# Turning and ReLU of the smallest expert blocks moved to the vector engine, with their first product by column halves (fp32 sigmoid attention and mixture of experts, one core)

## The chip, the core and the metric

The kernel runs on one core of a Trainium2 chip. Five engines work beside each other, each with an instruction queue of its own that it takes in order: TensorE (PE; its weight loads are counted apart as PEld), VectorE (DVE), ScalarE (ACT), GpSimd (POOL) and SyncE (SP), which here issues the plain transfers. An engine waits for another through semaphores. Matmul results land in PSUM, in banks of 512 fp32 numbers for each of 128 partitions; everything else lies in SBUF. The metric is the device time of one execution in microseconds (us), lower is better.

## What is computed

```python
scores = 1/sqrt(64) * q @ k.T - log(448)      # 8 x 12 heads, 448 x 64
x = sigmoid(scores) @ v                       # -> 3584 tokens x 768
out = x.copy()
for tokens with x @ w_skip > 0:
    e    = argmax(x @ w_gate)                 # one of 8 experts
    gate = softmax(x @ w_gate)[e]
    out  = x + gate * (relu(x @ w1[e]) @ w2[e])   # 768 -> 1024 -> 768
```

All of it is fp32.

## The kernel before

Up to about 322 us the kernel does attention and routing; the first two blocks of 128 tokens of the fullest expert are done at its end. Then a loop takes the rest block by block, one expert after the other. Which blocks there are is known only at run time, so each turn of the loop branches, on each engine, to one of four arms: FULL (a block of up to 128 tokens), SPLIT (the same, and the weights of the next expert, which lie there raw, are turned into pairs of a high and a low part on the side), HALF (up to 64 tokens) and FEW (up to 32 tokens). With the data used here there are 14 blocks in the loop, five of them FEW: four come behind a FULL block and one behind a SPLIT block; the last FEW block is the last of the program.

FULL and SPLIT form each product as three products of high and low parts. `gemm1` (L516) gives the hidden layer in `ph`, `relu` (L525, ACT) takes it to `hs`, `turn_h` (L530, PE) and `split_h` (L535 ACT, L536 DVE) turn and split it, `gemm2` (L543) gives the result in `py`: 48 matmuls of 384 columns, for each of 8 slices of the hidden layer three products, each for the two output halves. `weigh_sum` (L1316, DVE, twice) scales the halves of `py` by the gate into `ys`, `put` (POOL, L1281 to L1296 and the scatter, L570) adds them to the output in memory, `advance` (L1306, L1308, L1309, DVE) moves the block's records on. SPLIT has beside these the weights' conversions (L1225, L1231 on ACT; L1228, L1234 on DVE); the last four of L1234 stand at its very end, behind `advance`.

FEW uses the raw weights. It reads the tokens' transposed rows (`xf`) as weights of PE, 32 columns wide, so that four matmuls work side by side in four column groups of the array, and streams the expert's weights. In the order of the program:

- `take_rec` (L1313, DVE): copies the next block's record.
- First product (L1381, PE): 6 row tiles x 4 groups, 256 columns each, all in one bank `ph[0]`. Group g holds the hidden layer's columns 256g to 256g+255 of the 32 tokens in partitions 32g to 32g+31. An fp32 matmul counts as two passes: 48.
- ReLU (L1398, ACT) in two halves of 128 columns, from `ph[0]` into `hs`.
- `load_w1`: SP starts the transfers of the next expert's first weights. `turn_x` (L492): six PE transposes of the next block's rows, into `pxt`. `fetch` (POOL, L1259 to L1265 and the gathers L560 and L1111): gathers rows and record of the block after.
- Turn of the hidden layer: two PE transposes of 128 x 128 (L1407) into `pht[0]` and `ph[1]`, two copies on ACT (L1409) into `ht`.
- `ready_x`: `hi_x` (L498, ACT), `whole_x` (L1093, ACT), `lo_x` (L502, DVE) prepare the next block's rows out of `pxt`. `shift` (L1277, DVE) moves the list of coming blocks.
- Second product (L1381, PE): 4 rounds of 4 matmuls of 384 columns, one for each group; groups 0 and 1 make output half 0, groups 2 and 3 half 1, each from half of the hidden layer. All land in one bank, `py[:, 0, :]`.
- Sums: ACT scales groups 0 and 2 (L1434), DVE scales groups 1 and 3 and adds (L1436). Then `put` and `advance`.

A scheduler doesn't move instructions here: within an arm each engine's instructions stand in the order of the code.

Of the kernel before, what the change touches and what calls it, by code (L numbers as in the profile page):

```python
# [10 lines left out]
F32 = mybir.dt.float32  # L11
# [4 lines left out]
ALU = mybir.AluOpType  # L16
# [7 lines left out]
def kernel(  # L24
# [513 lines left out]
    def gemm2(j, hh, hl, py):  # L538
        h, m = divmod(j, 4)
        js = slice(m * P, (m + 1) * P)  # L540
        for n, (a, w) in enumerate(((hh, wh2), (hh, wl2), (hl, wh2))):
            for o in range(2):
                last = nc.tensor.matmul(  # L543
                    py[:, o, :H2],
                    a[h][:, js],
                    w[j][:, o * H2 : (o + 1) * H2],
                    start=(j == 0 and n == 0),
                    stop=(j == NK2 - 1 and n == 2),
                )
        return last  # L550

# [585 lines left out]
    pxt = [ps_b.tile([P, 512], F32, tag="b", name="pxt0"), new_t("pxt1")]  # L1137
    for h in range(2):
        turn_x(xc, h, pxt[h])
        hi_x(h, pxt[h], xh)  # L1140
# [58 lines left out]
    py = new_s("py")  # L1199
# [118 lines left out]
    def block(i, last):  # L1318
# [48 lines left out]
        for o in range(2):  # L1367
            weigh_sum(ys[:, o * H2 : (o + 1) * H2], py[:, o, :H2], recs[:, 0, 0:1])
# [6 lines left out]
    def few(i):  # L1375

        nx = next_expert(ds(i + 2, 1))
        take_rec()
# [11 lines left out]
        Q1 = FF // 4  # L1390
        for j in range(NK1):
            for g in range(4):
                s = slice((g % 2) * Q1, (g % 2 + 1) * Q1)
                quarter(ph[0], g, Q1, xf[:, j, :SM], raw1[j][g // 2][:, s], j, NK1)
        turned = (pht[0], ph[1])
        parts = [slice(c * P, (c + 1) * P) for c in range(2)]
        for s in parts:
            nc.scalar.activation(hs[:, s], ph[0][:, s], AF.Relu)  # L1398
# [6 lines left out]
        ht4 = ht[:, : 8 * SM].rearrange("p (c g t) -> p c g t", c=2, g=4)  # L1405
        for s, p in zip(parts, turned):
            nc.tensor.transpose(p[:, :P], hs[:, s], ident)  # L1407
        for s, p in zip(parts, turned):
            nc.scalar.activation(ht[:, s], p[:, :P], AF.Copy)  # L1409
# [3 lines left out]
        for n, j in enumerate((0, 2, 1, 3)):  # L1413
            for g in range(4):
                o, h = g // 2, g % 2
                m = j + h * (NK2 // 2)
                quarter(
                    py[:, 0, :],
                    g,
                    H2,  # L1420
                    ht4[:, j % 2, 2 * h + j // 2, :],
                    raw2[m][:, o * H2 : (o + 1) * H2],
# [135 lines left out]
```

## Time and profile before

| | |
|---|---|
| time, median of 3 runs | 525.33 us (525.12 to 526.49) |
| time of the profiled execution | 528.89 us |
| its span, first to last instruction | 526.5 us |
| mean granted PE clock | 0.993 |
| busy: PE, DVE, ACT, POOL | 97%, 56%, 53%, 49% |
| PE's matmuls at L1381, first products of the 5 FEW blocks | 14.1 us |
| PE's matmuls at L1381, second products of the 5 FEW blocks | 14.5 us |
| ReLU of the FEW blocks on ACT (L1398), 10 instructions | 2.2 us |

Times of the trace count from the first instruction. The chain of waits goes back from the last instruction, at each step to what released it. A timeline lists an engine's instructions with start, length, and in brackets the engine's idle time ahead and what ended it. "L1381" is a line of the kernel, and names such as `py<-raw,ht` are its tiles. Groups give busy time and, behind it, the mean ns of one instruction. The five FEW blocks begin on PE at 403.3, 429.5, 455.7, 481.8 and 507.4 us.

### The profile page before, as it was taken

What the parts mean: (1) busy time and instruction counts of PE and PEld (TensorE: products, weight loads), DVE (VectorE), ACT (ScalarE), POOL (GpSimd) and SP (SyncE); (2) the same over time, 40 slices, a digit from 0 to 9 for tenths busy, and PEclk for the clock granted to TensorE, in tenths of its full rate; (3) what the DMA queues carried; (4) which work ended last, traced back from release to release, by engine and by line L of the source; (5) the groups of instructions that cost most, each with busy time, mean ns of one, the idle gap of its engine ahead of it and who ended that gap; (6) DMA issues with size and microseconds to landing.
All of it is one profiled execution on the core that took longest, in us unless ns stands there. A gap on an engine that the chain in (4) does not pass through costs nothing.

```text
span 526.5 us, 14852 instructions
## 1 busy us (share of the span) xinstructions
PE 509.3 (97%) x4793; PEld 333.8 (63%) x4794; DVE 296.0 (56%) x721; ACT 280.8 (53%) x485; POOL 257.1 (49%) x404
## 2 busy tenths in 40 slices
PE   8999999999999999999999999999999999999991
PEld 6664545545545446555446988948577777778870
DVE  4556857658667677586775952962122222259422
ACT  5776776767767667677664212932212323268231
POOL 4523553533566766766663341553324444445643
PEclk9999999999999999999999999999999999999997
DMA  8998787897999999999865024979393959595941
GB/s 207 218 240 192 167 184 158 180 179 169 195 206 232 220 196 212 211 205 211 188 117 114 2 92 133 386 220 336 88 390 113 348 202 348 188 341 217 356 150 32
DMA packets 140288, 107.21 MB, mean 204 GB/s; under 512 B 97099, under 2 KB 112731, under 8 KB 140240
## 3 DMA queue, kind: packets, MB, share of 16 engines
q1 hardware_dynamic: 134000, 97.66, 70.0%
q0 software_dynamic: 4576, 8.65, 7.2%
q8 instruction: 30, 0.49, 0.4%
q10 hardware_dynamic: 1664, 0.26, 0.3%
q14 instruction: 18, 0.15, 0.1%
HBM read 98.49 MB, written 17.56 MB: 220 GB/s over the span
## 4 chain that ended last, share of the span: by engine, by line
PE 91%; DVE 3%; ACT 1%; DMA 1%; SPq 1%; issue 1%; POOLq 0%; ACTq 0%; POOL 0%; DVEq 0%
PE s L212 24%; PE pa L240 22%; PE ph L516 11%; PE py L543 11%; PE b_ph L516 3%; PE b_py L543 3%; PE py L1381 3%; PE ph L1381 2%; PE py L1448 2%; PE ph L1448 2%; PE pxt L492 2%; PE pl L280 1%; PE pht L530 1%; SPq L263 1%; PE pg L297 1%
## 5 line engine op out<-in xcount | busy, mean ns | idle before, releaser
L232 ACT ACTIVATE at<-s,bias 128x896 f32<-128x896 f32 (+1 forms) x191 | 173.4, 913 | 81.2 <-PE s L212 70.7
L212 PE MATMUL s<-x 64*64 64x448 f32 (+1 forms) x1528 | 163.9, 497 | 0.9 <-DVE sel L407 0.6
L240 PE MATMUL pa<-at,v 64*64 64x448 f32 (+1 forms) x1536 | 161.7, 489 | 0.0
L176 POOL COPY kq<-kq 32x896 f32<-32x896 f32 (+1 forms) x96 | 87.3, 910 | 92.2 <-DMA kq<-in_q_dram 52.2
L212 PEld LDWEIGHTS s<-x 64*64 64x64 f32 x1528 | 78.3, 191 | 54.3 <-issue 28.0
L240 PEld LDWEIGHTS pa<-at,v 64*64 64x64 f32 x1536 | 60.7, 133 | 56.3 <-issue 48.7
L194 DVE STREAM_TRANSPOSE x<-kq 128x448 f32<-128x448 f32 x94 | 80.9, 934 | 4.9 <-POOL kq L176 4.9
L250 DVE TENSOR_TENSOR xt<-xt,pa 128x448 f32<-128x448 f32 x48 | 29.7, 619 | 53.9 <-ACT xt L669 53.9
L414 POOL DMA_INDIRECT lst<-rec,idx x32 | 31.5, 983 | 17.6 <-DVE xt L250 5.4
L486 POOL TENSOR_TENSOR wl<-wr,wh 128x384 fp32r<-128x384 f32 (+1 forms) x28 | 31.2, 1124 | 15.1 <-DVE wh L485 9.2
L255 DVE STREAM_TRANSPOSE y<-xt 128x448 f32<-128x448 f32 x48 | 31.0, 645 | 5.5 <-DMA out_dram<-y 4.1
L570 POOL DMA_INDIRECT out_dram<-ys,rp x15 | 23.7, 1578 | 16.6 <-issue 8.4
L536 DVE TENSOR_TENSOR hl<-pht,hh 128x512 fp32r<-128x512 f32 x14 | 9.7, 689 | 37.0 <-ACT hh L535 30.0
L543 PE MATMUL py<-wh,hh 128*128 128x384 f32 x112 | 29.8, 347 | 0.0
L525 ACT ACTIVATE hs<-ph 128x512 f32<-128x512 f32 x14 | 8.3, 596 | 39.7 <-PE ph L516 31.7
L543 PE MATMUL py<-wh,hl 128*128 128x384 f32 x112 | 28.8, 338 | 0.0
L543 PE MATMUL py<-wl,hh 128*128 128x384 f32 x112 | 28.7, 337 | 0.0
L502 DVE TENSOR_TENSOR xl<-pxt,xh 128x384 fp32r<-128x384 f32 x30 | 15.3, 551 | 20.4 <-ACT xf L1093 8.3
L516 PE MATMUL ph<-wl,xh 128*128 128x512 f32 x84 | 26.6, 403 | 0.0
L669 ACT ACTIVATE xt<-pa 128x448 f32<-128x448 f32 x48 | 25.7, 536 | 0.8 <-PE pa L240 0.8
L516 PE MATMUL ph<-wh,xh 128*128 128x512 f32 x84 | 25.7, 402 | 0.0
L1316 DVE TENSOR_SCALAR ys<-py,recs 128x384 f32<-128x384 f32 (+1 forms) x18 | 10.4, 611 | 25.8 <-PE py L543 20.7
(275 smaller groups left out, 691.6 us busy)
## 6 DMA issues: line engine op xcount, KB each, us to landing
raw<-in_moe_w_dram SPq DMA_DIRECT2D x64, 768.0 KB
v<-in_v_dram SPq DMA_DIRECT2D x48, 256.0 KB
out_dram<-y SPq DMA_DIRECT2D x192, 56.0 KB
kq<-in_k_dram SPq DMA_DIRECT2D x46, 224.0 KB
kq<-in_q_dram SPq DMA_DIRECT2D x46, 224.0 KB
wr<-in_moe_w_dram SPq DMA_DIRECT2D x12, 256.0 KB
wr<-in_moe_w_dram SPq DMA_DIRECT2D x16, 192.0 KB
lst<-fill SPq DMA_DIRECT2D x4, 464.0 KB
```

The source lines that it names most:

```text
L176: nc.gpsimd.tensor_copy(a[BT:, :, :, :BT], a[:BT, :, :, BT:])
L194: nc.vector.transpose(xs[:, n].rearrange("p (r j) -> p j r", j=NJ), t.rearrange("p (j d) -> p j d", d=D)[:, :, :BT],)
L212: nc.tensor.matmul(sc[m * D : (m + 1) * D, j, : qs.stop - qs.start], xs[r, 0, first::NR7], xs[r, 1, qs], start=True, stop=True,)
L232: nc.scalar.activation(at[:, :, :n], sc[:, :, :n], AF.Sigmoid, bias=bias, scale=SCALE)
L240: nc.tensor.matmul(pa[j * D : (j + 1) * D, r, qs], vt[rs, j, r + c if c < 3 else 3 * (1 - r), :], at[rs, j, : qs.stop - qs.start], start=( ...
L250: nc.vector.tensor_tensor(x, x, pa[:, 1, :S], op=ALU.add)
L255: nc.vector.transpose(y, xts[b][:, hp, :])
L414: put = nc.gpsimd.indirect_dma_start(out=lst[:, :], out_offset=bass.IndirectOffsetOnAxis(ap=idx[:, c : c + 1], axis=0), in_=rec[:, c, :], ...
L486: nc.gpsimd.tensor_tensor(lo, r, hi, op=ALU.subtract)
L516: nc.tensor.matmul(ph[h], a[:, j * P : (j + 1) * P], w[j][h], start=(n == 0), stop=(n == len(t) - 1),)
L543: last = nc.tensor.matmul(py[:, o, :H2], a[h][:, js], w[j][:, o * H2 : (o + 1) * H2], start=(j == 0 and n == 0), stop=(j == NK2 - 1 and n ...
L1381: nc.tensor.matmul(dst[g * SM : (g + 1) * SM, :n], a, w, start=(j == 0), stop=(j == most - 1), tile_position=(0, g * SM),)
```

## The change

1. FEW's first product goes by column halves c: c=0 takes the first 512 columns of the hidden layer into `ph[0]`, c=1 the rest into `ph[1]`. Each of the 48 matmuls has 128 columns, read as 4 strips of 32 that lie 128 apart, so that group g holds the strips g, g+4 and so on. Blocks of 32 x 32 within `hs` are then all that has to be turned.
2. After each half DVE does the ReLU (a maximum with 0) out of PSUM and turns the 128 x 128 tile in blocks of 32 x 32 into `ht`. The two PE transposes, ACT's ReLU and ACT's copies go. `take_rec` stands behind the first half's turn.
3. The second product takes the slices of the hidden layer in another order, so that its first two rounds need half c=0 alone.
4. `py` is two tiles of one bank each in place of one of two banks. In FEW, groups 0 and 2 (read by ACT) write `py0`, groups 1 and 3 (read by DVE) `py1`. HALF uses `py0` alone. In FULL and SPLIT they are the two output halves, and the last slice of `gemm2` does half 0's three matmuls first.
5. `pxt` is one tile of two banks; at the end of the stage ahead of the loop both halves are turned first and taken by `hi_x` then.

The lines of the changed kernel stand 3 to 10 further down: `gemm2` L546, `take_rec` L1321, FEW's matmuls L1388, ReLU L1411, turn L1412, sums L1444 and L1446, `weigh_sum` L1324, the conversions L1242.

```diff
@@ -538,16 +538,22 @@
     def gemm2(j, hh, hl, py):
         h, m = divmod(j, 4)
         js = slice(m * P, (m + 1) * P)
-        for n, (a, w) in enumerate(((hh, wh2), (hh, wl2), (hl, wh2))):
-            for o in range(2):
-                last = nc.tensor.matmul(
-                    py[:, o, :H2],
-                    a[h][:, js],
-                    w[j][:, o * H2 : (o + 1) * H2],
-                    start=(j == 0 and n == 0),
-                    stop=(j == NK2 - 1 and n == 2),
-                )
+        parts = [(n, o) for n in range(3) for o in range(2)]
+        if j == NK2 - 1:
+            parts.sort(key=lambda t: t[1])
+        for n, o in parts:
+            a, w = ((hh, wh2), (hh, wl2), (hl, wh2))[n]
+            last = nc.tensor.matmul(
+                half_y(py, o),
+                a[h][:, js],
+                w[j][:, o * H2 : (o + 1) * H2],
+                start=(j == 0 and n == 0),
+                stop=(j == NK2 - 1 and n == 2),
+            )
         return last
+
+    def half_y(py, o):
+        return py[o][:, :H2] if isinstance(py, list) else py[:, o, :H2]
 
     def finish(ys, py, gate, x):
         for o in range(2):
@@ -1134,9 +1140,11 @@
     turn0(1)
     for j in range(2, NK2 - 3):
         gemm2(j, hh0, hl0, py)
-    pxt = [ps_b.tile([P, 512], F32, tag="b", name="pxt0"), new_t("pxt1")]
+    pxt2 = new_s("pxt")
+    pxt = [pxt2[:, h, :] for h in range(2)]
     for h in range(2):
         turn_x(xc, h, pxt[h])
+    for h in range(2):
         hi_x(h, pxt[h], xh)
     for h in range(2):
         whole_x(h, [slice(j, j + 1) for j in range(3)])
@@ -1196,7 +1204,7 @@
     raw2 = [raw2g[j // 2][:, j % 2, :] for j in range(NK2)]
 
     ph = [new_t(f"ph{h}") for h in range(2)]
-    py = new_s("py")
+    py = [new_t("py0"), ps_b.tile([P, 512], F32, tag="b", name="py1")]
     pht2 = new_s("pht")
     pht = [pht2[:, h, :] for h in range(2)]
 
@@ -1365,7 +1373,7 @@
         else:
             shift(dve)
         for o in range(2):
-            weigh_sum(ys[:, o * H2 : (o + 1) * H2], py[:, o, :H2], recs[:, 0, 0:1])
+            weigh_sum(ys[:, o * H2 : (o + 1) * H2], half_y(py, o), recs[:, 0, 0:1])
         put(P, last)
         advance(1 if last else 2)
         if last:
@@ -1375,7 +1383,6 @@
     def few(i):
 
         nx = next_expert(ds(i + 2, 1))
-        take_rec()
 
         def quarter(dst, g, n, a, w, j, most):
             nc.tensor.matmul(
@@ -1387,39 +1394,42 @@
                 tile_position=(0, g * SM),
             )
 
-        Q1 = FF // 4
-        for j in range(NK1):
-            for g in range(4):
-                s = slice((g % 2) * Q1, (g % 2 + 1) * Q1)
-                quarter(ph[0], g, Q1, xf[:, j, :SM], raw1[j][g // 2][:, s], j, NK1)
-        turned = (pht[0], ph[1])
-        parts = [slice(c * P, (c + 1) * P) for c in range(2)]
-        for s in parts:
-            nc.scalar.activation(hs[:, s], ph[0][:, s], AF.Relu)
+        split = [slice(c * P, (c + 1) * P) for c in range(2)]
+        for c, s in enumerate(split):
+            for j in range(NK1):
+                cols = raw1[j][c].rearrange("p (m g f) -> p g m f", g=4, f=SM)
+                for g in range(4):
+                    quarter(
+                        ph[c].rearrange("p (m f) -> p m f", f=SM)[:, :4],
+                        g,
+                        4,
+                        xf[:, j, :SM],
+                        cols[:, g],
+                        j,
+                        NK1,
+                    )
+            nc.vector.tensor_scalar(hs[:, s], ph[c][:, :P], 0.0, None, op0=ALU.max)
+            nc.vector.transpose(ht[:, s], hs[:, s])
+            if c == 0:
+                take_rec()
         for h in range(2):
             for g in range(2):
                 load_w1(g, h, nx)
         for h in range(2):
             turn_x(xn, h, pxt[h])
         fetch()
-        ht4 = ht[:, : 8 * SM].rearrange("p (c g t) -> p c g t", c=2, g=4)
-        for s, p in zip(parts, turned):
-            nc.tensor.transpose(p[:, :P], hs[:, s], ident)
-        for s, p in zip(parts, turned):
-            nc.scalar.activation(ht[:, s], p[:, :P], AF.Copy)
         ready_x()
         shift(dve)
 
-        for n, j in enumerate((0, 2, 1, 3)):
+        for n, m in enumerate((0, 1, 4, 5)):
             for g in range(4):
-                o, h = g // 2, g % 2
-                m = j + h * (NK2 // 2)
+                o, k = g // 2, m + 2 * (g % 2)
                 quarter(
-                    py[:, 0, :],
+                    py[g % 2],
                     g,
                     H2,
-                    ht4[:, j % 2, 2 * h + j // 2, :],
-                    raw2[m][:, o * H2 : (o + 1) * H2],
+                    ht[:, k * SM : (k + 1) * SM],
+                    raw2[k][:, o * H2 : (o + 1) * H2],
                     n,
                     NK2 // 2,
                 )
...
```

On VectorE, at the end of the SPLIT arm and the start of the FEW arm behind it, before (L1234: conversions of weights, the last three of four; L1313: `take_rec`; L502: `lo_x`; rows without a tile, such as REGISTER_ALU and ISA, are small instructions of the engine's sequencer):

```order
L1234 TENSOR_TENSOR wl_5_129<-raw_2_4371,wh_5_121 128x768
L1234 REGISTER_ALU
L1234 TENSOR_TENSOR wl_6_130<-raw_3_4372,wh_6_122 128x768
L1234 REGISTER_ALU
L1234 TENSOR_TENSOR wl_7_131<-raw_3_4372,wh_7_123 128x768
L1522 UNCONDITIONAL_BRANCH
L1313 COPY recs<-rn 128x2
L502 ISA
L502 TENSOR_TENSOR xl<-pxt_4302,xh 128x384
```

The same place now:

```order
L1242 TENSOR_TENSOR wl_6_130<-raw_3_4371,wh_6_122 128x768
L1242 REGISTER_ALU
L1242 TENSOR_TENSOR wl_7_131<-raw_3_4371,wh_7_123 128x768
L1532 UNCONDITIONAL_BRANCH
L1411 ISA
L1411 TENSOR_SCALAR hs<-ph_4372 128x128
L1412 ISA
L1412 STREAM_TRANSPOSE ht<-hs 128x128
L1321 COPY recs<-rn 128x2
L1411 ISA
L1411 TENSOR_SCALAR hs<-ph_4373 128x128
L1412 REGISTER_ALU
```

The conversions stay where they were; the ReLU and the turn of FEW now stand behind them on the same engine, and `take_rec` behind the first turn. Where a FULL block comes before, `advance` stands in the conversions' place.

On TensorE, the last slice of `gemm2` and the start of FEW, before (wh_7 and wl_7 are the high and low part of the last slice's weights; x2 is the two output halves, one behind the other):

```order
L543 MATMUL py<-wh_7_123,hh_4352 128x384 x2
L543 MATMUL py<-wl_7_131,hh_4352 128x384 x2
L543 MATMUL py<-wh_7_123,hl_4354 128x384 x2
L1522 UNCONDITIONAL_BRANCH
L1381 REGISTER_ALU
L1381 MATMUL ph_4373<-raw_0_0_4348,xf 32x256 x2
L1381 MATMUL ph_4373<-raw_1_0_4366,xf 32x256 x2
```

And now:

```order
L546 MATMUL py_4374<-wh_7_123,hh_4351 128x384
L546 MATMUL py_4374<-wl_7_131,hh_4351 128x384
L546 MATMUL py_4374<-wh_7_123,hl_4353 128x384
L546 MATMUL py_4375<-wh_7_123,hh_4351 128x384
L546 MATMUL py_4375<-wl_7_131,hh_4351 128x384
L546 MATMUL py_4375<-wh_7_123,hl_4353 128x384
L1532 UNCONDITIONAL_BRANCH
L1388 REGISTER_ALU
L1388 MATMUL ph_4372<-raw_0_0_4347,xf 32x128 x4
```

The last matmul of output half 0 has moved ahead of the three of half 1, and the first product starts with four matmuls into the bank of half c=0 where two by two of the columns' halves alternated.

More of the change, by code (lines that the diff above doesn't have):

```diff
@@ L1431, in few @@
                 s = slice(o * H2, (o + 1) * H2)
-                p = py[g * SM : (g + 1) * SM, 0, :H2]
+                p = py[m][g * SM : (g + 1) * SM, :H2]
                 if not m:
@@ L1486, in half @@
                 side(
-                    py[:, 0, :],
+                    py[0],
                     o,
@@ L1498, in half @@
             s = slice(o * H2, (o + 1) * H2)
-            weigh_sum(ys[:MD, s], py[o * MD : (o + 1) * MD, 0, :H2], recs[:MD, 0, 0:1])
+            weigh_sum(ys[:MD, s], py[0][o * MD : (o + 1) * MD, :H2], recs[:MD, 0, 0:1])
         put(MD)
```

## The prediction

> **What bounds the kernel now.** I read the page first, then the chain of waits over the loop of blocks, then engine timelines around one FEW block of each kind. The page says that TensorE is the bound:
>
> ```profile
> PE 509.3 (97%) x4793; PEld 333.8 (63%) x4794; DVE 296.0 (56%) x721; ACT 280.8 (53%) x485; POOL 257.1 (49%) x404
> PE 91%; DVE 3%; ACT 1%; DMA 1%; SPq 1%; issue 1%; POOLq 0%; ACTq 0%; POOL 0%; DVEq 0%
> ```
>
> The first line is busy time by engine, the second the share of each in the chain that ended last. Time can be won only in the few places where PE waits, and lost wherever new work makes it wait. The chain through one FEW block shows such a place:
>
> ```profile
> 403.32 2.73 PE ph L1381 x48
> 406.05 0.85 PE pxt L492 x6
> 406.90 0.29 ACT hs L1398
> 407.33 0.32 PE pht L1407
> 407.66 0.29 ACT ht L1409
> 408.04 2.91 PE py L1381 x32
> 410.95 2.06 PE ph L516 x8
> ```
>
> Columns: start, length, work. The first product ends at 406.05, six transposes of the next block's rows cover until 406.90, and from there to 408.04 the chain goes through ReLU on ACT, a turn on PE and a copy on ACT: 1.14 us in which PE does 0.32 of work, and that work exists only for the turning. The second product then leads straight into the next block. Between the start of the first product and that of the second lie 4.72 us. The FEW blocks at 429.49 and 455.66 read the same to 0.01 (starts of the two products):
>
> ```profile
> 429.49 2.73 PE ph L1381 x48
> 434.22 2.91 PE py L1381 x32
> 455.66 2.73 PE ph L1381 x48
> 460.37 2.91 PE py L1381 x32
> ```
>
> Two further FEW blocks differ: the one at 481.75 follows a SPLIT block, and the last one, at 507.41, ends the program. So the sum has three equal terms and two of their own. What the new work meets on VectorE decides all of them.
>
> **The change, part by part.** *Three FEW blocks behind a FULL block.* VectorE, which now gets ReLU and turn, comes out of the FULL block so:
>
> ```profile
> 403.42 1.14 DVE L1316 TENSOR_SCALAR ys<-py,recs 128x384 f32<-128x384 f32 x2 [4.14 <-PE py L543]
> 405.00 0.15 DVE L1309 CAST rid<-recs 128x1 int32<-128x1 f32 x1
> 407.06 0.17 DVE L1313 COPY recs<-rn 128x2 f32<-128x2 f32 x1 [1.91 <-issue]
> ```
>
> The two sums of the FULL block wait for PE's last matmul; bookkeeping ends at 405.15; then 1.91 us pass in which VectorE waits for nothing the profile shows (leaving one arm of the loop and entering the next), and its first instruction of FEW starts at 407.06, later than PE's transposes end. With the change that first instruction is the ReLU. It can come earlier only by what the FULL block ends earlier, and that is the order of the last matmuls: those of output half 0 now stand ahead of half 1, and the sums have separate tiles. Rows of the old order:
>
> ```profile
> 402.45 0.52 PE L543 MATMUL py<-wl,hh 128*128 128x384 f32 x2
> 402.81 0.51 PE L543 MATMUL py<-wh,hl 128*128 128x384 f32 x2
> 403.25 2.80 PE L1381 MATMUL ph<-raw,xf 128*32 128x256 f32 x48
> ```
>
> Pairs start 0.36 apart, 0.18 a matmul; three matmuls are 0.53. Half 0 is complete 0.53 earlier, its sum (0.57) runs while PE finishes half 1, and VectorE is through 0.53 earlier: 407.06 - 0.53 = 406.53. The new arm has one more register instruction ahead; 0.1 for it (0 to 0.3): 406.63.
>
> Then ReLU out of PSUM and a turn in 32x32 blocks, neither shown at 128x128. The nearest groups, mean ns of one behind the busy time:
>
> ```profile
> L1316 DVE TENSOR_SCALAR ys<-py,recs 128x384 f32<-128x384 f32 x14 | 8.0, 611 | 20.7 <-PE py L543 20.7
> L1306 DVE COPY sv<-recs 128x2 f32<-128x2 f32 x24 | 2.7, 156 | 0.0
> L255 DVE STREAM_TRANSPOSE y<-xt 128x448 f32<-128x448 f32 x48 | 31.0, 645 | 5.5 <-DMA out_dram<-y 4.1
> ```
>
> Between 156 at 2 columns and 611 at 384 a straight line gives 0.31 us at 128; between 156 and 645 at 448 it gives the turn 0.29. The ends are 0.16 and 0.61 for the one, 0.16 and 0.65 for the other; I take the lines. [...]
>
> With 0.06 between the two and 0.15 to PE (in the chain it was 0.02 to 0.14) the second product starts at 406.63 + 0.31 + 0.06 + 0.29 + 0.15 = 407.44 instead of 408.04. That is 0.60 a block, 1.8 for three. Ends: 0.30 (register instruction and hand-over at their worst), and 1.04 where VectorE isn't late and PE goes on right behind its transposes at 406.90 with a hand-over of 0.1. ReLU and turn of the second half, with the record's copy (0.17) between, end at 408.27; the second product needs that half only in its third of four rounds, at 407.44 + 1.45 = 408.89: hidden. The record's copy itself then starts near 407.3 instead of 407.06. What waits for it is POOL's gather into the buffer it reads:
>
> ```profile
> 410.34 0.99 POOL L1111 DMA_INDIRECT rn<-lst,rx  x1 [0.31 <-issue]
> ```
>
> That starts 3 us behind, so it costs nothing.
>
> The first product has twice as many matmuls of half the width. Now 48 passes in 12 rounds of four take 2.73, 0.228 a round; at 128 columns a round streams in 0.114, and the weight load of the round behind it has to fit beside it:
>
> ```profile
> L1381 PEld LDWEIGHTS ph<-raw,xf 128*32 128x32 f32 x240 | 7.2, 110 | 5.7 <-issue 1.6
> 419.97 0.66 PE pxt L492 x6
> ```
>
> 110 ns just fits, and six transposes of 128 columns, each with its own load, take 0.11 apiece. I count 2.73 to 3.2, and nothing on the path: PE has 407.44 - 406.90 = 0.54 to spare while VectorE is the later one. Without that cover it would cost up to 0.5 a block. Two PE transposes and four operations of ACT go, so ACT starts hi_x some 1.2 earlier, which nothing waits for. The two-bank tile for the transposes orders hi_x behind all six; ACT is free, so nothing.
>
> *The last block.* PE's end is not the end here:
>
> ```profile
> 512.16 3.96 PE py L1381 x32
> 513.05 1.06 POOL L560 DMA_INDIRECT xn<-out_dram,rp  x1 [0.74 <-PE py L1381]
> 514.42 0.99 POOL L1111 DMA_INDIRECT rn<-lst,rx  x1 [0.31 <-issue]
> 516.27 1.17 ACT L1434 ACTIVATE yt<-py,recs 32x384 f32<-32x384 f32 x2 [2.48 <-PE py L1381]
> 517.48 1.26 DVE L1436 SCALAR_TENSOR_TENSOR yt<-py,recs,yt 32x384 f32<-32x384 f32 x2 [2.52 <-ACT yt L1434]
> 515.07:518.85 3.78, 0.00 (x0) 0.00 (x0) 1.34 (x5) 1.15 (x2) 1.35 (x5) 1.00 0.06 18
> 518.87:526.50 7.63, 0.00 (x0) 0.00 (x0) 0.40 (x4) 0.00 (x0) 2.22 (x4) 0.50 0.10 13
> ```
>
> The last matmul ends at 515.07 (none in the window behind it), yet ACT's sums begin at 516.27, shortly after POOL's second gather. PE's 0.6 is therefore mostly not passed on: 0.1 (0 to 0.6). VectorE's sums waited until both of ACT's were done; with one tile for each engine, the first needs only the first of ACT, half of 1.17 earlier: 0.6. Together 0.7, ends 0.1 and 1.3.
>
> *The block behind SPLIT.* There VectorE holds work of the SPLIT block, ahead of the new work in its queue:
>
> ```profile
> 484.91 3.56 DVE L1234 TENSOR_TENSOR wl<-raw,wh 128x768 fp32r<-128x768 f32 x4
> 488.39 0.16 DVE L1313 COPY recs<-rn 128x2 f32<-128x2 f32 x1
> 481.75 2.87 PE L1381 MATMUL ph<-raw,xf 128*32 128x256 f32 x48
> 484.55 0.88 PE L492 MATMUL pxt<-ident,xn 128*128 128x128 f32 x6
> 485.96 2.91 PE L1381 MATMUL py<-raw,ht 128*32 128x384 f32 x32 [0.20 <-DVE wl L1234]
> ```
>
> Four conversions of weights run to 488.39, and before, FEW needed nothing of VectorE until then. Now its ReLU stands behind them: 488.39 + 0.31 + 0.06 + 0.29 + 0.15 = 489.20 for the second product, against 485.96. PE's transposes end at 485.43, nothing else can cover, and everything behind on PE's queue waits: 3.24 (3.0 to 3.6).
>
> Sum: -1.80 - 0.70 + 3.24 = +0.74. The profiled execution took 528.89, its span 526.5; the span would be 527.2. The median of the runs is 525.33, 0.7% under the profiled one, too little to scale a difference of 0.74: 526.1.
>
> **The rivals.** *VectorE isn't late (A).* If the 1.91 us of "issue" shrink, because they wait for PE's branch and not for code of the arm, the second product follows PE's transposes directly: 3 x 1.04 + 0.7 to 1.3 against 3.24, that is -0.6 to -1.2, 524.2 to 524.8. Against it: the same 1.91 stands ahead of the copy in the trace, and nothing in it is named.
>
> *The clock drops in the block behind SPLIT (B, slower).* PE would do nothing from 485.43 to 489.20, 3.77 us. In the tail the granted clock is 1.00 for 3.78 us behind the last matmul and 0.50 from there (the two windows above). If the gap becomes longer than that 3.78, by 0.01 or more, the second product runs at half clock: up to 2.91 more, 529.0. For it: the two lengths are equal to 0.01, and any cost that I have put too low comes in here. Against: the last of the six transposes may count as busy to its very end. [...]
>
> *The first product pays for its instructions (C).* If loads of 110 ns can't run beside streams of 114, 24 rounds of 0.224 take 5.38: the second product at 403.32 + 5.38 + 0.85 = 409.55, 1.51 later in three blocks; the last +1.5 and -0.6; behind SPLIT as forecast. 4.5 + 0.9 + 3.2 = 8.7: 534.0. The six transposes at 0.11 apiece speak against it.
>
> **How the numbers follow.** A measurement of this kernel can tell 0.3% from no change, 1.6 us: 523.75 to 526.9. The forecast has 0.56; with three blocks at 0.45 to 0.75, the last at 0.4 to 1.1 and SPLIT's at 3.0 to 3.5 its own range is 525.0 to 527.1. A has 0.16, B 0.19, C 0.06, and 0.03 are left for the gain without SPLIT's loss, about 523. B, C and the upper end of the forecast (0.08) lie beyond 526.9: 0.33; faster by more 0.05; the rest, 0.62, within. The range from A's best, 524.2, to most of B's, 528.6, leaves out C, the top of B and some of the unknown, under 2 in 10.
>
> **What would show it right or wrong.** In the trace of the changed kernel: VectorE's ReLU starts near 406.6 in the first FEW block, about 3.3 behind the start of PE's first product, and PE's second product about 4.1 behind it (4.72 before); behind SPLIT the ReLU follows the fourth conversion without a gap and PE shows one idle stretch of some 3.8, whose releaser is VectorE's turn, with the granted clock at 1.00; the first product lasts 2.7 to 3.2; in the tail VectorE's first sum overlaps ACT's second. It would be wrong if PE's second product starts 3.6 behind the first (A), if the second product behind SPLIT takes more than 4 us (B), if the first product takes 5 us (C), or if the ReLU doesn't wait for the conversions.

## The result and the profile after

| | before | changed |
|---|---|---|
| time, median of 9 runs each | 524.95 us | 529.15 us |
| ratio | | 1.0081 (95%: 1.0063 to 1.0099) |
| span of the profiled execution | 526.5 us | 527.4 us |
| of it from the loop's first matmul (L516) on | 203.4 us | 205.0 us |
| mean granted PE clock | 0.993 | 0.991 |

The change costs 4.2 us. 526.1 was forecast, in a range from 524.2 to 528.6; the measured 529.15 lies above it. The two traces differ by only 1.6 us in the loop; where the rest lies took experiments to find, and it begins with what the first trace of the kernel before did not tell: it was an execution of 528.89 us, and the runs it stood for took 525.

The chain of waits of the changed kernel through the first FEW block (start, length, work):

```profile
402.83 2.81 PE ph L1388 x96
405.64 0.27 PE pxt L492
406.10 0.30 DVE hs L1411
406.50 0.09 DVE ht L1412
406.73 0.14 DVE recs L1321
407.06 2.91 PE py L1388 x32
```

ReLU and turn on DVE have taken the place of ACT's and PE's steps. From the start of the first product to that of the second it is 4.23 us where it was 4.72: 0.49 won, 0.60 forecast. (A start on the chain can lie up to 0.08 behind the one in a timeline, which gives 4.30 and 4.80 for the same two; each comparison below keeps to one of the views.) The twice 48 passes take 2.81, as good as no more than the 2.73 of before. DVE's timeline at the same place, with idle time ahead and what ended it in brackets:

```profile
402.40 1.14 DVE L1324 TENSOR_SCALAR ys<-py,recs 128x384 f32<-128x384 f32 x2 [3.25 <-PE py L546]
403.97 0.15 DVE L1317 CAST rid<-recs 128x1 int32<-128x1 f32 x1
406.10 0.29 DVE L1411 TENSOR_SCALAR hs<-ph 128x128 f32<-128x128 f32 x1 [1.97 <-PE pxt L492]
406.50 0.31 DVE L1412 STREAM_TRANSPOSE ht<-hs 128x128 f32<-128x128 f32 x1
```

The sums start 0.43 ahead of the first product where they started 0.10 behind it, the idle time between the arms is 1.97 (1.91 before), ReLU and turn take 0.29 and 0.31 (0.31 and 0.29 in the forecast). The releaser in the bracket is only the event that lay nearest; half c=0 had been done for 1.9 us.

Behind SPLIT:

```profile
482.95 3.56 DVE L1242 TENSOR_TENSOR wl<-raw,wh 128x768 fp32r<-128x768 f32 x4
486.43 0.28 DVE L1411 TENSOR_SCALAR hs<-ph 128x128 f32<-128x128 f32 x1
486.82 0.31 DVE L1412 STREAM_TRANSPOSE ht<-hs 128x128 f32<-128x128 f32 x1
```

```profile
479.86 1.93 PE L1388 MATMUL ph<-raw,xf 128*32 128x128 f32 x40
482.09 1.84 PE L1388 MATMUL ph<-raw,xf 128*32 128x128 f32 x56 [0.30 <-ACT wh L1239]
483.86 0.87 PE L492 MATMUL pxt<-ident,xn 128*128 128x128 f32 x6
487.38 4.56 PE L1388 MATMUL py<-raw,ht 128*32 128x384 f32 x32 [2.65 <-DVE recs L1321]
```

The ReLU follows the fourth conversion without a gap, and the second product starts 7.52 behind the first instead of 4.21: 3.31 lost, 3.24 forecast. But then it takes 4.56 where it took 2.91. Windows over the gap and the product, and over the part of the product with the lowered clock (busy time of PE, PEld, DVE, ACT and POOL, then the granted PE clock, DMA share, GB/s):

```profile
483.86:487.38 3.52, 0.88 (x10) 0.67 (x7) 3.42 (x8) 1.57 (x8) 2.89 (x5) 1.00 0.95 328
487.38:491.94 4.56, 4.56 (x33) 2.63 (x33) 1.57 (x6) 0.00 (x0) 2.65 (x6) 0.63 0.97 284
487.47:490.89 3.42, 3.42 (x24) 2.23 (x27) 1.51 (x5) 0.00 (x0) 2.31 (x6) 0.50 0.94 295
```

0.63 over the product: the clock was halved for 3.42 us of it. That is the rival called B, at 1.65 us. A thing that nobody forecast is in the two HALF blocks; here the first of them:

```profile
340.97 5.30 PE ph L1458 x24
347.40 0.39 ACT ht L1487
347.99 5.38 PE py L1458 x32
```

7.02 from product to product, against 6.85 before (341.75 to 348.60):

```profile
341.75 5.30 PE ph L1448 x24
348.12 0.39 ACT ht L1477
348.60 5.38 PE py L1448 x32
```

The hand-over from ACT's copy to PE went from 0.09 to 0.20, which is 0.11 of the 0.17.

The tail of the changed kernel:

```profile
514.71 2.96 PE py L1388 x32
517.79 0.58 ACT yt L1444
518.39 0.05 DVE yt L1446
```

By the timelines ACT's first sum follows PE's last matmul by 0.18, and DVE's first sum no longer waits for ACT's second. Before, ACT's first sum came 1.21 behind PE's end, shortly after POOL's second gather, as the prediction noted. That gather ends here 0.87 behind PE's end (0.35 before), and the 1.0 us are gone all the same.

### The profile page after: what moved, and what is told of

It is laid out like the page before. It is cut to its first block, busy times and chain, and to the rows that moved or that the text cites. A ratio compares the mean times of both kernels' runs of the same rounds, so it can differ in the third digit from the quotient of the medians.

```text
span 527.4 us, 15259 instructions
## 1 busy us (share of the span) xinstructions
PE 509.0 (97%) x5023; PEld 343.0 (65%) x5024; DVE 302.6 (57%) x741; ACT 276.8 (52%) x465; POOL 257.9 (49%) x404
## 4 chain that ended last, share of the span: by engine, by line
PE 92%; DVE 3%; issue 2%; ACT 1%; DMA 1%; DVEq 0%; POOLq 0%; POOL 0%; ACTq 0%
PE s L212 24%; PE pa L240 23%; PE ph L516 11%; PE py L546 11%; PE b_ph L516 3%; PE b_py L546 3%; PE py L1388 3%; PE ph L1388 2%; PE py L1458 2%; PE ph L1458 2%; PE pl L280 2%; PE pxt L492 2%; PE pht L530 1%; PE pg L297 1%; DMA kq_first<-in_q_dram 1%
## 5 line engine op out<-in xcount | busy, mean ns | idle before, releaser
L212 PE MATMUL s<-x 64*64 64x448 f32 (+1 forms) x1528 | 170.2, 496 | 0.6 <-DVE sel L407 0.3
L240 PE MATMUL pa<-at,v 64*64 64x448 f32 (+1 forms) x1536 | 168.6, 489 | 0.0
L212 PEld LDWEIGHTS s<-x 64*64 64x64 f32 x1528 | 83.7, 191 | 49.9 <-issue 27.2
L240 PEld LDWEIGHTS pa<-at,v 64*64 64x64 f32 x1536 | 66.4, 133 | 55.2 <-issue 46.1
L498 ACT ACTIVATE xh<-pxt 128x384 fp32r<-128x384 f32 x30 | 13.1, 491 | 41.9 <-PE pxt L492 38.9
L546 PE MATMUL py<-wh,hh 128*128 128x384 f32 x112 | 30.9, 347 | 0.0
L546 PE MATMUL py<-wh,hl 128*128 128x384 f32 x112 | 30.0, 338 | 0.0
L546 PE MATMUL py<-wl,hh 128*128 128x384 f32 x112 | 29.8, 337 | 0.0
L516 PE MATMUL ph<-wl,xh 128*128 128x512 f32 x84 | 26.5, 402 | 0.0
L516 PE MATMUL ph<-wh,xh 128*128 128x512 f32 x84 | 25.8, 403 | 0.2 <-DVEq L1537 0.2
L502 DVE TENSOR_TENSOR xl<-pxt,xh 128x384 fp32r<-128x384 f32 x30 | 15.3, 550 | 18.7 <-ACT xf L1099 16.6
```

Of the source, the lines that this page charges most:

```text
L212: nc.tensor.matmul(sc[m * D : (m + 1) * D, j, : qs.stop - qs.start], xs[r, 0, first::NR7], xs[r, 1, qs], start=True, stop=True,)
L240: nc.tensor.matmul(pa[j * D : (j + 1) * D, r, qs], vt[rs, j, r + c if c < 3 else 3 * (1 - r), :], at[rs, j, : qs.stop - qs.start], start=( ...
L516: nc.tensor.matmul(ph[h], a[:, j * P : (j + 1) * P], w[j][h], start=(n == 0), stop=(n == len(t) - 1),)
L546: last = nc.tensor.matmul(half_y(py, o), a[h][:, js], w[j][:, o * H2 : (o + 1) * H2], start=(j == 0 and n == 0), stop=(j == NK2 - 1 and n ...
```

## The experiments

The expectations weigh named theories. Theory Q: the loss is in the FEW block behind SPLIT, by DVE's queue and the clock that falls while PE waits. Rival S: the change also costs some 2 us elsewhere. Later came theory P, on what differs between executions. The runs e, the runs f and g, and the runs h were made on three chips, one each, and on each the kernel before took 529.0 or 529.1, not the 525 of the result.

**e0, the kernel before again.** No edit.

> The kernel before, unchanged, to see where its usual time lies: its first profiled execution took 528.89 us, 4 us over the median of its runs (524.95), so the two traces (loop of blocks 203.2 us before, 205.0 after) differ by less than the times do (4.2). Theory Q (the loss lies in the FEW block behind SPLIT: 3.3 us of waiting on VectorE's queue and 1.65 of halved clock): the loop takes 203.2 again and the stages ahead of it about 320. Rival S (the change also costs some 2 us elsewhere, in the stages that it seems not to touch): the stages ahead of the loop are 2 to 3 us shorter than the 322.4 of the changed kernel in most runs of the kernel before and never in the changed one. Time 525.

529.88 against 529.06 for other runs of the same program, ratio 1.0014 (95%: 1.0003 to 1.0025, as in every bracket behind a ratio below): what two equal programs can differ by here. The loop took 203.4 again, and started at 323.1. So a trace of 526.5 belongs to runs of 529, and not to the 525 of the result.

**e2, two of the last four conversions left out.**

```diff
-            for j in range(4, NK2):
+            for j in range(4, NK2 - 2):
                 lo2(j)
```

> The changed kernel with two of SPLIT's last four conversions left out (slices 6 and 7 keep the low parts of the expert before). It tells queue and clock apart. If the clock falls because PE does no matmul for longer than some window (3.5 us in the changed kernel without its transposes), the gap shortened by 1.8 no longer makes it fall: 1.8 + 1.65 = 3.4 us less, about 525.7, second product behind SPLIT 2.9 long at clock 1.00. If the clock falls for another reason (any gap, or the two banks), only the 1.8 is saved: 527.3, second product still about 4.5 long.

529.38, ratio 1.0009 (0.9998 to 1.0020). PE behind SPLIT:

```profile
482.85 1.84 PE L1388 MATMUL ph<-raw,xf 128*32 128x128 f32 x56 [0.31 <-ACT wh L1239]
484.62 0.87 PE L492 MATMUL pxt<-ident,xn 128*128 128x128 f32 x6
487.10 2.91 PE L1388 MATMUL py<-raw,ht 128*32 128x384 f32 x32 [1.61 <-DVE recs L1321]
```

```profile
484.70:487.10 2.40, 0.79 (x6) 0.58 (x7) 1.77 (x6) 1.17 (x6) 2.10 (x5) 1.00 0.97 306
487.10:490.00 2.90, 2.90 (x33) 1.90 (x33) 1.70 (x6) 0.40 (x4) 1.80 (x6) 1.00 0.94 304
```

With 2.4 us between the last matmul of the first product and the second product, the clock stays at 1.00 and the product takes 2.91. With 3.45 by the same count (the changed kernel) it falls. So here the shorter gap spared the clock, and Q is borne out in that; that the length is not all, the paragraph on the clock below shows. The time is 2.6 us less than that of the changed kernel on the next chip (f1), where Q expected 3.4: the wait itself shrank by 1.04 only, not 1.8; f3 tells why.

**e1, all four left out.** The two lines of the loop above go altogether.

> The changed kernel without SPLIT's last four conversions of weights on VectorE (slices 4 to 7 keep the low parts of the expert before; their values are not what the reference computes). Theory Q: the ReLU of the FEW block behind SPLIT is no longer held up, its second product starts 4.2 behind the first as in the other FEW blocks (7.5 in the changed kernel), at full clock, 2.9 long (4.56): 5.0 us less, about 524.2. Rival S: the same 5.0 cannot appear if the loss lies elsewhere; 529 less what the waiting alone costs, and the clock still falls.

532.54, ratio 1.0063 (1.0046 to 1.0079): 3.5 slower than the kernel before, where 5 less than the changed one was expected. The trace shows that the edit had moved a wait. The second SPLIT block took 20.56 us instead of 18.5:

```profile
463.88 1.64 PE ph L516 x4
465.52 0.56 ACT yt L1441
466.10 0.62 DVE yt L1443
466.86 5.60 PE ph L516 x23
```

PE's `gemm1` stands still until DVE has done the sums of the FEW block ahead, which it doesn't need. It goes with the number of DVE's instructions at SPLIT's end, four fewer here: f3, which keeps that number, has the block at 18.5 again. How the wait came to move no run shows. So the time of e1 says nothing on the four conversions. Its trace does: without any of them the second product behind SPLIT still starts 5.97 behind the first, and not 4.2; it takes 2.91, at full clock.

**f3, the four conversions cut short.** So the next kernel kept the number of instructions:

```diff
             for j in range(4, NK2):
-                lo2(j)
+                few_cols = slice(0, 8)
+                nc.vector.tensor_tensor(
+                    wl2[j][:, few_cols], raw2[j][:, few_cols], wh2[j][:, few_cols], op=ALU.subtract
+                )
```

> The changed kernel with SPLIT's last four conversions cut to 8 of 768 columns each, so that the queue has the same instructions and every wait counts the same, but VectorE is free some 3 us earlier (the other columns keep the low parts of the expert before). Theory Q: the second product behind SPLIT starts 4.9 to 5.2 behind the first (7.5), held by the first product's own 4.1 and the transposes, at full clock: 2.5 + 1.65 = 4.1 us less than f1. Rival S: at most the 2.5 less, and f1's distance to the kernel before does not close.

530.31, ratio to the kernel before 1.0018 (1.0007 to 1.0030), 1.7 less than f1 (531.99), and not 4.1. DVE's timeline:

```profile
485.15 0.15 DVE L1317 CAST rid<-recs 128x1 int32<-128x1 f32 x1
485.37 0.59 DVE L1382 TENSOR_TENSOR wl<-raw,wh 128x8 fp32r<-128x8 f32 x4
488.03 0.29 DVE L1414 TENSOR_SCALAR hs<-ph 128x128 f32<-128x128 f32 x1 [2.07 <-PE pxt L492]
```

PE behind it:

```profile
488.99 2.91 PE L1391 MATMUL py<-raw,ht 128*32 128x384 f32 x32 [1.22 <-DVE recs L1321]
```

The conversions end at 485.96, and the ReLU comes 2.07 later. In between stand branches, the loading of the loop's scalars and semaphores; in the result's trace of the changed kernel the same small instructions lie between 482.97 and 485.69, under the four conversions (482.95 to 486.51), and the ReLU follows these without a gap. The second product starts 6.60 behind the first (7.51 in f1), at full length 2.91. So of the 3.3 lost behind SPLIT the conversions answer for 0.9; the other 2.4 are there without them. About half of these is DVE, which leaves SPLIT late and enters FEW 2 us after: PE waits 1.22 for it behind its transposes. About the other half is PE's first product, which takes 4.1 here instead of 2.9, as the halves reach the last row tile before ACT is through with SPLIT's conversions (the bracket with ACT's wh in e2's rows). The expectation counted the first product and left out the step into the arm, although the prediction had used its 1.91 for the FULL blocks.

**e3, the banks alone**, in the kernel before:

```diff
-    py = new_s("py")
+    py = [new_t("py0"), ps_b.tile([P, 512], F32, tag="b", name="py1")]
...
+        if j == NK2 - 1:
+            parts.sort(key=lambda t: t[1])
...
-                    py[:, 0, :],
+                    py[g % 2],
```

> The kernel before with the two one-bank sum tiles, the order of the last slice and the two-bank tile of the transposes, but FEW's first product, ReLU and turn as they were. Theory Q: no loss behind SPLIT, the tail shorter by 0.6 to 1.6, the three HALF blocks longer by up to 0.17 each as in the changed kernel: 0.3 to 1.5 faster, 523.5 to 524.7. Rival S: the two tiles carry the unexplained 2 us, 526 to 527.5.

527.80, ratio 0.9975 (0.9966 to 0.9985): 1.3 faster than the kernel before, and the fastest of the kernels here that do all the work. FEW's second product needs nothing of DVE here, so PE doesn't wait for it behind SPLIT (4.32 from product to product, 4.21 before). The HALF blocks (two; the expectation's three was a slip) take 0.10 longer each.

**h3, the halves alone**, the counterpart:

```diff
-    py = [new_t("py0"), ps_b.tile([P, 512], F32, tag="b", name="py1")]
+    py = new_s("py")
...
-        if j == NK2 - 1:
-            parts.sort(key=lambda t: t[1])
```

> The changed kernel with one two-bank sum tile again, the old order of the last slice and the old tiles for the transposes: FEW's first product by halves, ReLU and turn on VectorE alone. Theory Q: the banks alone gave 1.3 us, so this is 4 to 5 us slower than the kernel before (ratio 1.008 to 1.010): VectorE leaves FULL 0.5 later, so FEW behind FULL starts its second product 4.8 behind the first and gains nothing; behind SPLIT the 3.3 and the halved clock remain. Rival: the parts don't add, and it is as slow as the changed kernel (1.006).

535.90, ratio 1.0111 (1.0094 to 1.0127), 5.9 us by the ratio where 4 to 5 were expected. The clock takes more than counted: with one tile, DVE comes 0.4 later still (4.68 from product to product behind FULL, 7.86 behind SPLIT), the gap behind SPLIT grows, and the second product there takes 5.47. A HALF block takes 6.98, between the 6.92 of before and the 7.08 to 7.13 of the changed kernel, so a part of HALF's loss comes without the two tiles. The parts don't add: against f2's 203.5 the loop is 0.4 shorter in e3, 6.3 longer here, and 2.6 longer with both (f1). The banks are worth more where DVE is what PE waits for: 3.7 us of the loop with the halves (6.3 less 2.6), 0.4 without.

**f1 and f2, both kernels on one chip**, unchanged.

> The changed kernel, unchanged, on the same chip as f2 and f3. Open is why it was timed 4.2 us (0.8%) slower while its trace has only 1.9 us more in the loop of blocks than that of the kernel before (202.0 against 203.2 to PE's last matmul and tail: 205.0 against 203.2), which was taken on another chip. Theory Q (FEW behind SPLIT: waiting and clock): ratio about 1.0035 to 1.005 here, loop 205. Rival S (something outside the loop costs 2 us besides): ratio 1.008 again, and the stages ahead of the loop over 2 us longer than in f2.

> The kernel before, unchanged, for a trace from the same chip as f1. Both theories: ratio 1.000 within 0.0015, which is how far two sets of runs of one program stood apart. Theory Q: start of the loop at the same time as in f1 within 1 us. Rival S: 2 us or more earlier than in f1.

531.99, ratio 1.0062 (1.0040 to 1.0083), and 529.20, ratio 1.0001 (0.9992 to 1.0010). The ratio lies above the 1.0035 to 1.005 that Q expected, though its interval reaches into it. The loops start at 323.7 and 323.4 and take 206.1 and 203.5 us; the spans differ by 2.9, the times by 2.8. On one chip, trace and time agree, and S, with 2 us outside the loop, falls. A smaller part of it stays open: over all traces the loop starts at 323.0 to 323.4 in the kernel before (four traces), and at 322.4 to 324.9 in the changed kernel and its variants. PE of the changed kernel on this chip:

```profile
404.16 2.65 PE L1388 MATMUL ph<-raw,xf 128*32 128x128 f32 x86
407.07 0.61 PE L1388 MATMUL ph<-raw,xf 128*32 128x128 f32 x10 [0.26 <-issue]
408.46 2.91 PE L1388 MATMUL py<-raw,ht 128*32 128x384 f32 x32
```

The same program as in the result, but here PE stops ten passes before the end of the first product, and nothing is named; the product takes 3.52 instead of the 2.88 of the result's timeline. The kernel before has no such stop, but its ReLU is late (its first product and second product, its ReLU, and POOL's scatter):

```profile
403.58 2.80 PE L1381 MATMUL ph<-raw,xf 128*32 128x256 f32 x48
408.38 2.95 PE L1381 MATMUL py<-raw,ht 128*32 128x384 f32 x32 [0.20 <-ACT ht L1409]
```

```profile
407.25 0.45 ACT L1398 ACTIVATE hs<-ph 128x128 f32<-128x128 f32 x2 [8.73 <-PE pxt L492]
```

```profile
405.75 1.63 POOL L570 DMA_INDIRECT out_dram<-ys,rp  x1 [0.59 <-issue]
```

The first product ends at 406.38, ACT has been free for 8 us, and the ReLU starts 0.87 later, while POOL issues the scatter of the FULL block. The trace also has the times at which PE's signals reach the semaphore by which other engines wait for it. Those around this scatter in f2, in f1, and in the changed kernel's trace of the result (the longest pause, and where it begins):

```
f2  before   scatter 405.75 to 407.38   longest pause of PE's signals 0.68 from 406.37
f1  changed  scatter 405.80 to 407.43   longest pause of PE's signals 1.12 from 405.95
    changed  scatter 404.40 to 406.03   longest pause of PE's signals 0.18 from 405.73
```

Theory P came from this: under POOL's indirect DMAs PE's signals are held up, 0.7 us at a time, in some executions, and what waits for a signal of PE is late by that; in the result's they are not (0.18 at the most under the scatters ahead of FEW). The times alone don't show it, because the traces with pauses lack a part of the records (f2 has 910 of 1002 signals, f1 1029 of 1112, the result's trace all 1112), so that a pause can hold signals that were not recorded. That the ReLU is late doesn't hang on these records.

**g1, halves with ReLU on ACT and turn on PE:**

```diff
-            nc.vector.tensor_scalar(hs[:, s], ph[c][:, :P], 0.0, None, op0=ALU.max)
-            nc.vector.transpose(ht[:, s], hs[:, s])
+            nc.scalar.activation(hs[:, s], ph[c][:, :P], AF.Relu)
...
+            nc.tensor.transpose(ph[c][:, 2 * P : 3 * P], hs[:, split[c]], ident)
+            nc.scalar.activation(ht[:, split[c]], ph[c][:, 2 * P : 3 * P], AF.Copy)
```

> The changed kernel with FEW's ReLU on ACT and the turn by two PE transposes and ACT copies again, but on column halves (contiguous strips of 128 columns for each group), so that ReLU of the first half runs under the second half's matmuls and VectorE has nothing of it. Theory Q: FEW behind FULL starts its second product about 4.0 behind the first (4.3 in the changed kernel, 4.8 before), FEW behind SPLIT about 5.2 (7.5 and 4.2; the first product by halves reaches the last row tile a microsecond earlier than ACT is done with SPLIT's conversions), no halved clock: 3.2 less behind FULL, 1.0 more behind SPLIT, tail 1.1 less than the kernel before: 0.5% faster. Rival S: 0.1% faster or none, since the banks cost what the FEW blocks give.

529.09, ratio 1.0008 (0.9994 to 1.0022): no gain, where 0.5% was expected. Behind SPLIT 5.28 as expected. Behind FULL 4.76 and not 4.0; the first product has the same stop there, and ends after 3.55:

```profile
403.79 2.53 PE ph L1388 x86
406.66 0.61 PE ph L1388 x10
408.55 2.72 PE py L1388 x32
```

The stop is here too, with contiguous strips, so it isn't the strided strips. It is not in e3, with 48 passes, where the scatter starts 1.64 into the product as in f1 and g1. The number of passes is not all either: h3 has 96, its scatter starts 2.17 into the product, and the product takes 2.88.

**h1 and h2, both kernels without the loop's scatters:**

```diff
         seen(ys, H2)
-        out_rows = scatter(rp[0][:n], ys[:n], ALU.add)
-        tc.declare_no_dep(out_rows.ins, group="got", across_iterations=True, reason="a token is in one block only")
-        tc.add_to_no_dep_group("put", out_rows.ins)
```

> The kernel before with the scatter of each block's rows left out of the loop (POOL's indirect DMA at the end of put; the rows of the loop's blocks never reach the output). Theory P: on these chips PE's signals to other engines are held up by about 0.7 us at a time while POOL issues an indirect DMA; in FEW behind FULL the scatter (1.63 us) runs across the end of the first product, and ACT's ReLU starts 0.65 late. Without it the ReLU starts 0.2 behind the first product and the second product 4.2 behind the first (4.8 with the scatter): 0.6 less in each of four FEW blocks, 2.4 us, and some from the end of the program, where the last scatter itself (some 5 us with its landing) goes as well: 7 us less. Rival: the ReLU is late for another reason (the arm's own code): 4.8 stays.

> The changed kernel with the same scatter left out. Theory P: VectorE, not PE's signal, is what its second product waits for, so 4.3 stays behind FULL, while the first product loses its pause (3.5 to 2.9): against h1 it is then 2 us worse than the two kernels are against each other with the scatter, 5 us slower than h1, as on the chip of the first timing (4.2). Rival: the distance between h1 and h2 is the same 3 us as between the kernels with the scatter.

h1 522.15, ratio 0.9880 (0.9862 to 0.9898); h2 528.04, ratio 0.9978 (0.9968 to 0.9988). In h1 the ReLU comes 0.22 behind the first product's end and the second product 4.16 behind the first:

```profile
403.17 2.80 PE L1378 MATMUL ph<-raw,xf 128*32 128x256 f32 x48
407.33 2.91 PE L1378 MATMUL py<-raw,ht 128*32 128x384 f32 x32 [0.20 <-ACT ht L1406]
```

```profile
406.19 0.45 ACT L1395 ACTIVATE hs<-ph 128x128 f32<-128x128 f32 x2 [8.09 <-PE ph L1378]
```

In h2 the stop in the first product is gone (2.86), and the second product still comes 4.31 behind the first, since DVE sets it. The two kernels are now 5.9 us apart, where they are 2.8 (f) or 3.6 (h4) apart with the scatter; by the traces 4.7 of the 5.9 lie in the loop (196.9 and 201.6 us), against 2.6 in f, and the rest ahead of it. P is borne out: the time that the change saved behind FULL was not the turning, but a lateness that the scatter causes. Without that, its way is 0.15 longer than the old one. That it is PE's signal that is late rests on the times of the signals above.

**h4, the changed kernel on a third chip.** No edit.

> The changed kernel once more. Theory P: where the kernel before takes 529 (PE's signals held up), ratio 1.006 with the last product ending 1.5 late; where it takes 525 (not held up), ratio 1.008 and a trace as in the first timing, with no gap in PE's signals over 0.5 us under POOL's scatters. Rival: the ratio doesn't go with the time of the kernel before.

532.61, ratio 1.0057 (1.0040 to 1.0074) with the kernel before at 529.0, the stop in the first product again (3.52), the second product behind SPLIT at 4.26. That fits P's first half. The loop takes 206.1 as in f1. Runs of 525 of the kernel before didn't come up again, so the second half rests on one trace, that of the result.

## Why the prediction was wrong

By f1 and f2, on one chip, starts from the timelines of both traces:

| term | forecast | f1 against f2 |
|---|---|---|
| three FEW blocks behind FULL | -1.80 | -1.50 (4.80 to 4.30 each) |
| last block: ACT's first sum earlier | -0.10 | -0.10 (8.93 to 8.83 behind the block's start) |
| last block: DVE's sums no longer behind ACT's second | -0.60 | -0.60 |
| FEW behind SPLIT: second product later | +3.24 | +3.30 |
| its second product at a lower clock | 0, as rival B | +1.26 |
| two HALF blocks | 0 | +0.37 |
| sum | +0.74 | +2.7 (the loops differ by 2.6) |

*Behind SPLIT.* The step was right, to 0.06, and so was the reading that four conversions stand ahead of the ReLU in DVE's queue. What it did not say is that more lies under them: with the conversions cut short, f3 still loses 2.4 of the 3.3.

*The clock.* This is the step that failed: the lower clock behind the wait, a term that the sum put at nothing. By f1 and f2 it is 1.26 of the 2.0 that the sum lacks; of the 3.5 that it lacks against the result's 4.2 it is 1.65, and the rest is argued below. B was worked out and then put at a chance of 0.19, because 3.78, read from one tail, was taken for a threshold, and the wait was counted from the end of PE's transposes (3.77). The tails of the other traces show that 3.78 is none. In f3, behind the last matmul at 517.57:

```profile
517.57:519.84 2.27, 0.00 (x0) 0.00 (x0) 0.40 (x4) 0.68 (x2) 1.36 (x3) 1.00 0.21 52
519.86:528.80 8.94, 0.00 (x0) 0.00 (x0) 1.64 (x7) 0.45 (x1) 2.85 (x6) 0.50 0.09 11
```

Over all traces the clock falls 2.28 (f3) to 5.38 (e3) behind the last matmul of the program. Behind SPLIT it fell in each of the five traces with 3.41 to 3.79 between matmuls and in none of the three with 1.89 to 2.48 (e1, e2, f3). The changes of one trace lie whole multiples of 3.41 apart: it is halved for 3.42 in four traces and for 6.83 in h3, and the fall in the tail comes 34.13 behind the fall behind SPLIT in the result (37.55 in h3). So, by these traces, the gap's length counts, and also where it lies in a beat of 3.41 us; f3's tail fell after less than the 2.41 that e2 was spared with, so e2's full clock may be luck in part. That the wait counts from the end of PE's transposes was the author's assumption: in the changed kernel the clock fell 2.73 behind the last transpose and 3.54 behind the last matmul of the first product, and no run tells the two apart.

The price was 1.26 to 1.65, and 2.56 in h3, not the 2.91 that was named as the most. It is about half of the halved time that falls on the product: 3.42, 2.87, 2.91 and 2.73 us of it in the result, h2, h4 and f1 cost 1.65, 1.34, 1.35 and 1.26. In h3 the whole product, 5.47, ran at the lower clock.

*Behind FULL.* The arithmetic held (0.49 to 0.50 for 0.60; the hand-overs from ReLU to turn and from turn to PE took 0.05 and 0.10 more), and the reason was wrong. The prediction read the 1.14 us between PE's transposes and the second product as ReLU, turn and copy. 0.65 of that was ACT's ReLU starting late, which goes with the scatter (h1). The kernel before showed it already: in its block behind SPLIT the ReLU starts 0.20 behind the first product instead of some 0.86, and the second product 4.21 behind the first instead of 4.80. Of the runs of 525 there is no trace, but their time, 4 us under the others, and the changed kernel's trace from the same comparison, with pauses of PE's signals of 0.18 at the most under the scatters ahead of FEW, say that nothing was there to be won: four blocks at +0.1 in place of -0.5. That would take 2.7 to 5.1, against 4.2 measured, and against 4.7 in the loops of h1 and h2. This part is argued from h1, h2 and one trace, not shown on those runs.

*The trace and the runs.* The prediction noted that the profiled execution was 0.7% over the median, and passed over it as "too little to scale". It was the sign that the trace held some 4 us that the timed runs had not; that they lay in the places that the change touches is the part that is argued.

*The tail.* Both terms came as forecast in f1 and f2. What keeps PE's gain from being passed on is PE's last signal: in f1 it arrives at 520.06, PE's last matmul having ended by the profile at 518.56, and ACT starts 0.12 behind it. The prediction saw only that ACT started shortly after POOL's second gather; in the result's trace that gather ends 0.87 behind the last matmul, the signal comes 0.06 behind it, and ACT isn't held up.

*HALF.* The prediction had no term for it. The two tiles alone add 0.10 a block (e3), the halves alone 0.06 (h3), both 0.16 to 0.21. Why the halves add anything there is not known.

*The first product* was rightly put at 2.7 to 3.2 with a cover of 0.54: it took 2.81, and 3.5 where the stop is, and even then didn't delay the second product behind FULL.

## What to carry to other kernels

When work is moved to an engine, look at what that engine does in every arm that can come before, and count the step into the arm (2.07 in f3) as well as the queue (3.56 in the result): with both there, only the longer showed. A wait of PE is priced at its length and then at the clock behind it (3.30 and 1.26 by f1 and f2), and one gap that went well (3.78 in the tail of the kernel before) is no threshold for the next (the clock fell behind 3.41 in h2). When a traced execution is slower than the runs it stands for (528.89 and 525 here), find out first where, for a change in that place may only win what the runs don't lose.

## What the runs showed of the hardware

- In the first trace of the kernel before, the records of PE's signals to its semaphore pause for 0.66 to 0.70 us under each of the four scatters ahead of a FEW block behind FULL (1.62 to 1.63 us of POOL each); under the first of them the pause was 0.68 in f2 and 1.12 in f1. In the result's trace of the changed kernel it is 0.18 at each of the four. Without the scatter (h1) the ReLU started 0.22 behind the end of the first product, against 0.87 in f2, and the program took 522.15 us against 529.0 (4.0 of it behind PE's last matmul, where the scatter at the end itself goes).
- In f1, g1 and h4, with 96 passes in the first product and the scatter 1.64 to 1.65 us into it, PE itself stopped and the product took 3.52, 3.55 and 3.52; in the result, with the same passes and the scatter as far in, it took 2.88. With 48 passes (e3, scatter 1.64 into it) the product took 2.80, with 96 and the scatter 2.17 into it (h3) 2.88, neither with a stop.
- The changes of the granted clock between 1.00 and 0.50 lay whole multiples of 3.41 us apart within a trace: 3.41 and 30.72 in the result's. It fell 2.28 (f3) to 5.38 us (e3) behind the last matmul, and behind SPLIT with every gap between matmuls of 3.41 (h2) to 3.79 (h3), with none of 1.89 to 2.48 (e1, e2, f3). In f3's tail the 3.41 us ahead of the fall still held 1.13 us of matmuls.
- From the last instruction of one arm to the first of FEW, DVE had 1.91 us of idle time in the kernel before and 1.97 in the changed one behind FULL, and 2.07 behind SPLIT in f3, where the conversions are short. Behind four conversions of 0.95 us each (the result) there was no gap, behind two (e2) 0.52.
- ReLU of 128 columns out of PSUM on DVE took 0.28 to 0.29 us, a turn of 128 x 128 in blocks of 32 x 32 0.31 (the result, f1, e2, f3).
